# Filler matmuls on a cleared tile, from TensorE's first moment to the first keys, in a windowed-attention and squared-ReLU kernel

## The chip, the cores and the metric

The kernel runs on one core of a Trainium2 chip. The metric is the device time in microseconds (us); lower is better. Four runs of the kernel before gave 293.84, 294.88, 294.56 and 294.54 us, so the median is 294.55 us.

## What is computed

Causal attention with a window of 64 keys over 8 batches, 8 heads, 576 positions and 64 values a head, and then a feed-forward layer with a squared ReLU on its 4608 tokens:

```python
scores = scale * np.matmul(q, k.transpose(0, 1, 3, 2))
rel = pos[:, None] - pos[None, :]
mask = (rel >= 0) & (rel < window)            # window = 64
scores = np.where(mask, scores, -1000000000.0)
attn = softmax of scores
x = (attn @ v), heads side by side             # 4608 x 512
h = np.maximum(x @ w_in, 0.0)                  # w_in 512 x 2048
return (h * h @ w_out)                         # w_out 2048 x 512
```

(The softmax line and the line for x are shortened here.) All inputs and the output are float32; the kernel multiplies in float16.

## The kernel before, in words

**Tiling.** The 4608 tokens are 36 tiles of 128. Two tiles make a pair, four make a group of 512 tokens. A pair's q and k come by one DMA each (`fetch_pair`, L124), v by one DMA a tile (`fetch_v`, L149), all in float32. Each tile is cast to float16 (`cast_k`, `cast_q`, `cast_v`, L269 and L267), q and k are transposed on TensorE through the identity (`T`, L363) and copied out of PSUM (`copy_kT`, `copy_qT`). `S_` (L413) multiplies keys and queries. For the first four tiles it starts from a bias that holds the mask: two matmuls of the identity with `minus` (L417). `expo` (L430) takes the exponential on ScalarE, `V` (L441) multiplies with the values, `norm` (L452: `rden`, `x_sb`) divides by the row sum on VectorE, `X` (L464) transposes the result and `copy_xT` puts it in place as `xT`. `shift_v` makes the copy of v that is shifted by 64 rows (`v_od`). `U` (L492) is the first feed-forward product of a pair, `relu` and `square` follow, and `O` and `out_seven` make the second product.

**Order.** Nothing is scheduled by a planner in the stretch that matters here. The string `FIRST` (L17) lists the opening work by hand, from left to right: `fv3` is the fetch of v of tile 3, `kc1/D` the cast of k of tile 1 on VectorE (`/D`; `/A` is ScalarE, nothing is GpSimd), `Tk0` the transposes of k of pair 0, `ck0` their copy, `S0` the scores of tile 0, `ea0` and `eb0` its two halves of the exponential, `V0`, `n0`, `X0`, `x0` the later steps of tile 0, `w3.0` the scaling of one piece of w_in. Each engine takes its own instructions strictly in this order. All DMAs are issued on SP's queue, in this order too.

**Fillers.** `W` followed by a number calls `warm` (L541). It takes the next PSUM buffer of two pools in turn and issues that many matmuls into it whose results nobody reads. Each multiplies the identity with the first 256 columns of `mask_first`:

```python
for _ in range(n):
    nc.tensor.matmul(ps[:, 0:256], ident[:],
                     mask_first[:].rearrange("p a r -> p (a r)")[:, 0:256],
                     start=True, stop=True)
```

The list holds `W10` ahead of the first keys, `W1` between the first transposes of k and q, `W6` ahead of `S0`, `W2` after `S1`, `W5` between `V0` and `V1`, `W7` after `Tq1` and `W8` after `X0`: 39 filler matmuls. The identity comes from GpSimd (L223). `mask_first` comes from GpSimd's `base` (L224 to L233), a copy and a clearing on VectorE (L245, L249). Ahead of those, VectorE runs 19 small memsets (L192, L238 to L241).

Of the kernel before, what the change touches and what calls it, by code (L numbers as in the profile page):

```python
# [10 lines left out]
FP16 = mybir.dt.float16  # L11
# [3 lines left out]

SQ_ACT = (0, 1, 4, 6, 8, 10, 12, 14)
FIRST = '''  # L17
fv3 fk0 fq0 W10 fv0 kc1/D kc0 fq1 Tk0 W1 fv1 qc1/A qc0 vc3/A Tq0 W6 vc0/D h0 vd0 cq0 fv2 ck0 fk1
qc2/A S0 S1 W2 vc1 ea0 fw3 vd3 fw2 eb0 vd1/D ea1 fw1 V0 W5 qc3/D eb1 vc2 fw0 h2 n0 vd2 V1 Tq1 W7
n1 kc2/A kc3 cq1 Tk1 X0 W8 ck1 x0 X1 S2 x1/A fv4 w3.0 w3.3/A S3 w3.1 ea2 w3.2 eb2 U0.7 ea3 V2 eb3  # L20
w2.2 U0.6 w2.3/A n2 w2.0/A V3 w2.1 r0.7 X2 n3 U0.5 r0.6 s0.7/A x2 X3 h4 U0.4 r0.5 x3 fk2 w1.0
s0.6/A U1.7 w1.1 w1.3/A s0.5 U1.5 r0.4 r1.7/D s0.4/A fq2 U1.6 w1.2 r1.5 s1.7 w0.0/A U0.2 w0.2 vc4
# [18 lines left out]
def kernel(  # L41
# [9 lines left out]
    nc = tc.nc  # L51
    B, H, S, D = q.shape
    NT, DM = out.shape
    DFF = moe_w_in.shape[1]
    P = 128
# [13 lines left out]
    const = ctx.enter_context(tc.tile_pool(name="const", bufs=1))  # L69
# [116 lines left out]

    def as_stage(ap, c=4):
        return ap.bitcast(FP32).rearrange("p (c n) -> p c n", c=c)


    tick_of = smallp.tile([P, 16], FP32, name="tick", tag="tick", bufs=1)
    nc.vector.memset(tick_of[:, 0:1], 0.0)  # L192
    nc.scalar.activation(out=tick_of[:, 1:2], in_=tick_of[:, 0:1], func=AF.Exp)

    wb_stage = as_stage(wb_all[:, 0:2].rearrange("p i k n -> p (i k n)"))
    hs_stage = as_stage(hs_all[:].rearrange("p i k n -> p (i k n)"))
    w_in_stage = [as_stage(early[:, 0:8].rearrange("p f t -> p (f t)")),
                  as_stage(early[:, 8:16].rearrange("p f t -> p (f t)")),
                  wb_stage, hs_stage]
# [22 lines left out]
    ident = const.tile([P, P], FP16, name="ident")  # L222
# [20 lines left out]
    def make_mask(name, first=None):  # L243
        m = const.tile([P, HP * 2, 64], FP16, name=name)
        nc.vector.tensor_copy(out=m[:], in_=base[:].rearrange("p (o r) -> p o r", o=1)  # L245
                              .to_broadcast([P, HP * 2, 64]))
        if first is not None:
            mm = m[:].rearrange("p (a b) r -> p a b r", b=2)
            nc.vector.memset(mm[0:64, :, first, :], 0.0)  # L249
        return m  # L250

    mask_first = make_mask("mask_first", 0)
# [104 lines left out]
    def either_pool():  # L357
        turns.append(len(turns) % 2)
        return ((ps_up, "ps_u"), (ps_out, "ps_o"))[turns[-1]]
# [181 lines left out]
    def warm(n):  # L541
        pool, tag = either_pool()
        ps = pool.tile([P, 512], FP32, name="warm", tag=tag)
        for _ in range(n):
            nc.tensor.matmul(ps[:, 0:256], ident[:],
                             mask_first[:].rearrange("p a r -> p (a r)")[:, 0:256],
                             start=True, stop=True)

    def w_out_sum(k0, kind):
        ks, kl = slice(k0, k0 + 2), slice(KH + k0, KH + k0 + 2)  # L550
# [34 lines left out]
    def out_seven(g):  # L585
# [118 lines left out]
        "V": V, "n": norm, "X": X, "x": copy_xT,   # L704
        "U": U, "r": relu, "s": square, "O": O, "oe": out_copy, "st": out_store,
        "ws": lambda kind, k0: w_out_sum(2 * k0, kind), "W": warm,
    }
    engines = {"A": nc.scalar, "D": nc.vector, "P": nc.gpsimd}
# [129 lines left out]
```

## Time and profile before

| what | us |
|---|---|
| median of four runs | 294.55 |
| lowest and highest run | 293.84, 294.88 |
| the profiled execution, its own time | 293.84 |
| its span, first to last instruction | 292.1 |
| outside the span | 1.7 |

| engine | busy us | share of the span |
|---|---|---|
| TensorE (PE), matmuls | 283.4 | 97% |
| TensorE, weight loads (PEld) | 195.6 | 67% |
| VectorE (DVE) | 213.4 | 73% |
| ScalarE (ACT) | 192.1 | 66% |
| GpSimd (POOL) | 112.2 | 38% |

The profiled execution is the fastest of the four runs. All times inside the profile count from its first instruction. A row of the timeline gives the start, the length from the first start to the last end, the engine, the line, the operation, the tiles (written <- read), the shape and the number of instructions that were merged. A bracket at its end gives the time that the engine sat idle before it and what ended that. Matmuls overlap in the records: each one's length includes its way through the array, so the distance from one start to the next is what a matmul costs in a stream. The lines that carry the argument are shown in the prediction.

### The profile page before, as it was taken

How to read it: one execution, taken by the hardware profiler on the slowest of the kernel's cores; microseconds unless marked ns; L12 is line 12 of the kernel's file. 1: busy time of each engine (PE TensorE's matmuls, PEld its weight loads, DVE VectorE, ACT ScalarE, POOL GpSimd, SP SyncE). 2: the span in 40 equal slices, each digit the busy share in tenths (PEclk: the TensorE clock that was granted, in tenths of full speed). 3: DMA queues.
4: the chain of work that ended last, by engine and by line, in shares of the span. 5: the costliest groups of instructions: out<-in, count | busy, mean ns of one | idle time of the engine just before them, and what ended most of it. 6: DMA issues, size and time to landing. Idle time of an engine off the chain costs nothing.

```text
span 292.1 us, 7468 instructions
## 1 busy us (share of the span) xinstructions
PE 283.4 (97%) x3039; PEld 195.6 (67%) x3039; DVE 213.4 (73%) x392; ACT 192.1 (66%) x304; POOL 112.2 (38%) x171
## 2 busy tenths in 40 slices
PE   3999999999999999999999999999999999999995
PEld 2678888755666666666666666666666666666684
DVE  3679999869968677766777687768876876555393
ACT  2779898968676666756675767575758575666500
POOL 2602877667338603324655726251356300000000
PEclk9999999999999999999999999999999999999999
DMA  7999999999799378899999999799979901300133
GB/s 211 291 394 319 271 250 280 375 259 244 214 224 213 70 214 186 187 188 260 238 244 192 228 225 181 176 237 213 227 159 267 180 2 49 133 0 2 72 108 110
DMA packets 151842, 57.64 MB, mean 197 GB/s; under 512 B 128256, under 2 KB 143616, under 8 KB 151808
## 3 DMA queue, kind: packets, MB, share of 16 engines
q1 hardware_dynamic: 151808, 57.16, 80.6%
q8 instruction: 24, 0.39, 0.5%
q14 instruction: 10, 0.08, 0.1%
HBM read 38.80 MB, written 9.44 MB: 165 GB/s over the span
## 4 chain that ended last, share of the span: by engine, by line
PE 80%; DVE 10%; DMA 3%; ACT 3%; SPq 2%; issue 1%; POOL 0%; POOLq 0%
PE hps L526 30%; PE opsC L614 10%; PE opsD L614 8%; PE hps L498 7%; PE opsA L614 6%; PE ops L574 5%; PE opsB L614 4%; PE av L448 3%; DVE hs_all L602 3%; PE sc L425 2%; DVE pm L436 2%; DMA v_st<-in_v_dram 2%; DVE x_sb L457 1%; DMA xT<-x_sb 1%; PE xt_ps L468 1%; SPq L130 1%
## 5 line engine op out<-in xcount | busy, mean ns | idle before, releaser
L526 PE MATMUL hps<-xT,w_in_sb 128*128 128x512 f16 x448 | 112.9, 379 | 0.4 <-DVE h L536 0.2
L530 ACT ACTIVATE hrelu<-hps 128x512 f32<-128x512 f32 x112 | 66.7, 597 | 63.7 <-PE hps L526 63.1
L614 PEld LDWEIGHTS <-h 128*128 128x128 f16 x624 | 60.4, 98 | 20.8 <-issue 0.2
L526 PEld LDWEIGHTS <-w_in_sb 128*128 128x128 f16 x448 | 42.2, 98 | 33.6 <-issue 0.6
L536 DVE SCALAR_TENSOR_TENSOR h<-hps,hrelu 128x512 f16<-128x512 f32 x54 | 37.2, 689 | 32.6 <-ACT hrelu L530 32.4
L269 POOL COPY v_od<-v_ev 64x512 f16<-64x512 f16 x54 | 38.8, 718 | 5.3 <-ACT v_ev L267 1.4
L431 ACT ACTIVATE pm<-sc 128x1024 f16<-128x1024 f32 (+1 forms) x40 | 35.4, 941 | 3.7 <-PE sc L425 3.7
L533 ACT ACTIVATE h<-hrelu 128x512 f16<-128x512 f32 x58 | 36.5, 629 | 1.6
L614 PE MATMUL opsA<-w_out_sb,h 128*128 128x256 f16 x240 | 31.0, 273 | 0.0
L614 PE MATMUL opsD<-wb_all,h 128*128 128x256 f16 x240 | 30.9, 273 | 0.0
L614 PEld LDWEIGHTS <-hs_all 128*128 128x128 f16 x256 | 25.0, 98 | 8.6
L498 PE MATMUL hps<-xT,w_in_sb 128*128 128x256 f16 x256 | 30.1, 273 | 0.0
L498 PEld LDWEIGHTS <-w_in_sb 128*128 128x128 f16 x256 | 24.2, 98 | 2.9
L457 DVE TENSOR_TENSOR x_sb<-av,rden 128x512 f16<-128x512 f32 x36 | 24.9, 692 | 1.2
L436 DVE TENSOR_TENSOR pm<-pm,mask_inner 128x1024 f16<-128x1024 f16 x25 | 20.5, 824 | 5.6 <-ACT pm L431 5.6
L269 POOL CAST k<-kq_st 128x512 f16<-128x512 f32 x17 | 10.4, 614 | 33.1 <-DMA kq_st<-in_k_dram 32.8
L269 POOL CAST q<-kq_st 128x512 f16<-128x512 f32 x22 | 14.5, 658 | 18.8 <-DMA kq_st<-in_q_dram 18.7
L636 DVE SCALAR_TENSOR_TENSOR osb_all<-opsD,u 128x512 f32<-128x512 f32 x14 | 9.7, 692 | 11.2 <-PE opsD L614 11.1
L614 PE MATMUL opsC<-w_out_sb,h 128*128 128x256 f16 x128 | 16.4, 273 | 0.0
L614 PE MATMUL opsB<-wb_all,hs_all 128*128 128x256 f16 x128 | 16.4, 273 | 0.0
L614 PE MATMUL opsC<-w_out_sb,hs_all 128*128 128x256 f16 x128 | 16.4, 273 | 0.0
L269 POOL CAST v_ev<-kq_st 128x512 f16<-128x512 f32 x16 | 11.2, 698 | 11.4 <-DMA kq_st<-in_v_dram 10.9
(103 smaller groups left out, 371.2 us busy)
## 6 DMA issues: line engine op xcount, KB each, us to landing
kq_st<-in_k_dram SPq DMA_DIRECT2D x26, 256.0 KB, 3.9
kq_st<-in_v_dram SPq DMA_DIRECT2D x24, 256.0 KB, 4.1
out_dram<-osb_all SPq DMA_DIRECT2D x12, 512.0 KB, 4.3
kq_st<-in_q_dram SPq DMA_DIRECT2D x18, 256.0 KB, 4.3
v_st<-in_v_dram SPq DMA_DIRECT2D x16, 256.0 KB, 5.6
k_st<-in_k_dram SPq DMA_DIRECT2D x7, 512.0 KB, 6.0
q_st<-in_q_dram SPq DMA_DIRECT2D x7, 512.0 KB, 5.9
out_dram<-osb_all SPq DMA_DIRECT2D x11, 256.0 KB, 2.8
```

Of the source, the lines that this page charges most:

```text
L269: eng.tensor_copy(out=out, in_=in_)
L431: nc.scalar.activation(out=pms[i][:, part], in_=scs[i][:, part], func=AF.Exp, scale=1.0 / float(D) ** 0.5)
L436: nc.vector.tensor_tensor(out=pms[i][:, part], in0=pms[i][:, part], in1=mask[:].rearrange("p (o a) r -> p o (a r)", o=1) .to_broadcast([P, ...
L457: nc.vector.tensor_tensor(out=xs[i // 2][:, i % 2], in0=avs[i][:, :, :, 0:D], in1=rden[:].to_broadcast([P, 2, 4, D]), op=ALU.mult)
L498: nc.tensor.matmul(hps[:, f, :], w_in_sb[:, c, (2 * j + f) * P:(2 * j + f + 1) * P], xT_of(p // 2)[:, n0:n0 + 2, c, :], start=(c == 0), st ...
L526: nc.tensor.matmul(hps[:], w_in_sb[:, c, f * P:(f + 1) * P], xT_of(g)[:, :, c, :], start=(c == 0), stop=(c == DMC - 1))
L530: nc.scalar.activation(out=hrelu[:], in_=hps[:], func=AF.Relu)
L533: later(2 if f == 0 else 0, lambda: nc.scalar.activation(out=h2_of(g)[:, f, :], in_=hrelu[:], func=AF.Square))
L536: nc.vector.scalar_tensor_tensor(out=h2_of(g)[:, f, :], in0=hps[:], scalar=0.0, in1=hrelu[:], op0=ALU.max, op1=ALU.mult)
L574: nc.tensor.matmul(ops_of[ts][:], h2s[0][:, f, ts * P:(ts + 1) * P], w_out_sb[:, f, :], start=(f == 0), stop=(f == FFC - 1))
L614: nc.tensor.matmul(rows_of(bank, m), a[:, kk, m * P:(m + 1) * P], w[:, kk], start=(first and kk == 0 and (m == 0 or bank in apart)), stop= ...
L636: nc.vector.scalar_tensor_tensor(out=dst, in0=banks[bank][:, ms], scalar=OUT_SCALE, in1=sums[add][:, ms], op0=ALU.mult, op1=ALU.add)
```

## The change

The tile `idle` (128 x 256, float16) is new. VectorE clears it ahead of its other work. Every filler multiplies this tile by its own first 128 columns; it no longer reads the identity or `mask_first`. Three counts in the list change: `W10` becomes `W25`, `W6` becomes `W12` and `W2` becomes `W4`, so there are 62 fillers instead of 39.

```diff
-fv3 fk0 fq0 W10 fv0 kc1/D kc0 fq1 Tk0 W1 fv1 qc1/A qc0 vc3/A Tq0 W6 vc0/D h0 vd0 cq0 fv2 ck0 fk1
-qc2/A S0 S1 W2 vc1 ea0 fw3 vd3 fw2 eb0 vd1/D ea1 fw1 V0 W5 qc3/D eb1 vc2 fw0 h2 n0 vd2 V1 Tq1 W7
+fv3 fk0 fq0 W25 fv0 kc1/D kc0 fq1 Tk0 W1 fv1 qc1/A qc0 vc3/A Tq0 W12 vc0/D h0 vd0 cq0 fv2 ck0 fk1
+qc2/A S0 S1 W4 vc1 ea0 fw3 vd3 fw2 eb0 vd1/D ea1 fw1 V0 W5 qc3/D eb1 vc2 fw0 h2 n0 vd2 V1 Tq1 W7
...
+    idle = const.tile([P, 256], FP16, name="idle")
+    nc.vector.memset(idle[:], 0.0)
+
+
     tick_of = smallp.tile([P, 16], FP32, name="tick", tag="tick", bufs=1)
     nc.vector.memset(tick_of[:, 0:1], 0.0)
...
-            nc.tensor.matmul(ps[:, 0:256], ident[:],
-                             mask_first[:].rearrange("p a r -> p (a r)")[:, 0:256],
-                             start=True, stop=True)
+            nc.tensor.matmul(ps[:, 0:256], idle[:, 0:P], idle[:], start=True, stop=True)
```

In the built program the order of all other instructions stays as it was on every engine. From the first `out_seven` on, the sums `p1` and `u` take other ones of the five slots that they share with the v tiles.

## The prediction

> **What bounds the kernel now.** I read the page first: busy time and slices.
>
> ```profile
> PE 283.4 (97%) x3039; PEld 195.6 (67%) x3039; DVE 213.4 (73%) x392; ACT 192.1 (66%) x304; POOL 112.2 (38%) x171
> ...
> PE   3999999999999999999999999999999999999995
> ...
> PEclk9999999999999999999999999999999999999999
> ```
>
> TensorE is busy from the second slice to the end, so the time is its stream plus its start. The change touches only the start. PEclk says full clock throughout, yet the timeline of the first 18 us shows that TensorE is not at full speed there:
>
> ```profile
> 2.72 2.29 PE L545 MATMUL warm<-mask_first,ident 128*128 128x256 f16 x10 [2.72 <-DVE mask_first L249]
> ...
> 6.97 1.03 PE L373 MATMUL kT_ps<-ident,k 128*128 128x128 f16 x8 [1.96 <-POOL k L269]
> ...
> 8.23 1.03 PE L373 MATMUL qT_ps<-ident,q 128*128 128x128 f16 x8
> ...
> 9.05 1.49 PE L545 MATMUL warm<-mask_first,ident 128*128 128x256 f16 x6
> ...
> 10.33 0.75 PE L417 MATMUL sc<-osb_all,ident 128*128 128x512 f16 x2
> ...
> 11.36 0.61 PE L417 MATMUL sc<-osb_all,ident 128*128 128x512 f16 x2
> ...
> 14.01 0.62 PE L373 MATMUL qT_ps<-ident,q 128*128 128x128 f16 x8
> ...
> 17.19 0.38 PE L468 MATMUL xt_ps<-ident,x_sb 128*128 128x128 f16 x4 [0.23 <-DVE xT L269]
> ```
>
> Eight transposes take 1.03 us at 6.97 and 8.23 but 0.62 at 14.01: from start to start 0.107 us against 0.056. A 256-column filler costs 0.213 us up to 10.33 and 0.109 from 12.24 on. So TensorE runs at half speed until about 10.65 (inside the pair of 10.33, whose first matmul takes 0.374 instead of 0.216), some 3.7 us after the transposes began. The burst of 2.72 to 4.80 was too short to end the half speed.
>
> Then I read who waits. The waits of TensorE in the first 60 us are three, two of them before any useful work:
>
> ```profile
> PE warm L545 <- DVE mask_first L249: 2.7, 1, 2.7
> PE kT_ps L373 <- POOL k L269: 2.0, 1, 2.0
> PE xt_ps L468 <- DVE xT L269: 0.2, 1, 0.2
> ```
>
> The third, at 17.19, is the last time that TensorE waits before its dense stream. The chain leads there, and not through the slow matmuls:
>
> ```profile
> 6.07 4.85 DMA v_st<-in_v_dram
> ...
> 11.04 0.62 POOL v_ev L269
> ...
> 11.68 0.28 DVE v_od L269
> ...
> 15.63 1.21 DVE qT L269
> 16.84 0.31 DVE xT L269
> ...
> 17.19 0.38 PE xt_ps L468 x4
> ```
>
> The v of tile 1 lands at 10.92. GpSimd casts it, and VectorE works ten instructions in a row without idling, 11.68 to 17.14, the last being `x0`. X1 starts 0.05 later. From 17.19 to 35 us the stream has no other gap but about 0.095 us where matmuls of another shape begin.
>
> **The change part by part.**
>
> *Clearing.* 128x256 float16 has the size of the kT memset at 8.87 (128x128 words, 0.17 us). It runs at 0.88, where VectorE's first memset stood, so the first filler starts at 0.88 + 0.17 + 0.05 = 1.10 instead of 2.72. Every early VectorE instruction moves by at most 0.17; the last ends near 3.4 instead of 3.21, and the next waits for a DMA until 6.02. Nothing of this is paid. If that cover were gone, it would cost 0.17. No DMA, no GpSimd and no SP instruction is moved.
>
> *W25.* At half speed 25 x 0.213 = 5.33 us, ending at 6.43. The keys are cast at 6.91, so this fits with 0.5 us to spare. If the clock rises 3.4 to 3.7 us after 1.10, as it did after 6.97, that is at 4.5 to 4.8: 16 or 17 fillers at 0.213, eight or nine at 0.109, ending near 5.6.
>
> *What rises.* [...] By the row alone (3.7 us after a start) TensorE is fast from 4.8. [...]
>
> *What is fast then.* The transposes of q still wait for GpSimd's cast until 8.23. They end 8 x (0.107 - 0.056) = 0.41 sooner, and VectorE's `cq0` starts at 9.04 instead of 9.30 (behind its memset). W12 costs 12 x 0.109 = 1.31, from 8.67 to 9.98, where W6 cost 1.28 and ended at 10.33. The bias pair costs 0.43 instead of 0.59. S0 starts near 10.51 instead of 11.02, the exponentials 0.5 sooner, W4 adds 2 x 0.109 = 0.22 while V0 waits for them, and V0 and V1 come about 0.5 sooner. Then it ends: k of tile 2 is cast at 14.15 when its DMA lands and k of tile 3 by 15.19 on GpSimd, so Tk1 gains 0.17 at most; X1 waits for `x0` at 17.14 as before. The wait at X1 grows from 0.40 to about 0.5. S2 follows X1. So against the profiled execution, 293.84, the sum is zero.
>
> *Where a gain remains.* The profiled execution is the fastest of four; the median is 0.71 above. [...] Slow work after 10.65 costs about half its length. [...] I take this for the main cause of the spread; this one trace cannot show it. With TensorE fast before 8 us in every run, the loss is gone: near 293.84, plus 0.15 for what else varies. Forecast 294.0. The bounds of this term are 0 (the spread has other causes) and -1.0 (the slowest run's whole excess).
>
> *Later slots.* The sums take other slots from 78 us on; the last v tile is read by 69.9, so no wait comes from it: zero.
>
> **The rivals.**
>
> *No change, 294.55.* The loss is hidden anyway: by the chain view VectorE and the v transfer set 17.19, and the spread comes from DMAs. For it: the chain as shown. [...] Range 294.2 to 294.9.
>
> [...]
>
> [...]
>
> **How the numbers follow.** Cases: gone spread 0.60 (own range 293.5 to 294.4), no change 0.25, window in the pause 0.09, zeros 0.06. About 0.3% (0.88 us) is what a measurement of this kernel can tell from no change, so faster means below 293.67 and slower above 295.43. Faster: a third of the first case, 0.20. Slower: the zeros and a remainder, 0.08. The range 293.4 to 294.9 takes in the first three and leaves out the last.
>
> **What would show it.** In the profile after: the first filler at 1.10 and W25 over before 6.5; transposes at 6.97 within about 0.62 us; S0 near 10.5; X1 still waiting for VectorE's `xT` near 17.2, with a longer wait; everything later as before; and runs that lie closer together. I am wrong if X1 comes clearly sooner, if the transposes at 6.97 take 1.03, or if the runs spread as before.

## The result, and the profile after

The changed kernel takes 294.0 us (median of 35 runs, 292.65 to 296.5), the kernel before 294.8 us in the same comparison (56 runs, 293.33 to 296.45). The ratio is 0.9982, 95% interval [0.9968, 0.9997]. That is a small gain, within the 0.3% that the prediction called no change; 294.0 was forecast. A second comparison (experiment 8) gave 0.9988 and does not rule out no change at all. The profiled execution took 293.67 us, its span is 291.8 us.

The timeline of the changed kernel over its first 20 us, its TensorE rows, beside those of before:

```profile
1.13 5.37 PE L549 MATMUL warm<-idle 128*128 128x256 f16 x25 [1.13 <-DVE tick L196]
...
6.59 0.62 PE L377 MATMUL kT_ps<-ident,k 128*128 128x128 f16 x8
...
7.89 0.62 PE L377 MATMUL qT_ps<-ident,q 128*128 128x128 f16 x8 [0.58 <-POOL q L273]
...
8.35 1.47 PE L549 MATMUL warm<-idle 128*128 128x256 f16 x12
...
10.19 0.41 PE L429 MATMUL sc<-qT,kT 64*128 64x64 f16 x16
...
16.74 0.38 PE L472 MATMUL xt_ps<-ident,x_sb 128*128 128x128 f16 x4 [0.24 <-DVE xT L273]
```

The fillers begin at 1.13 instead of 2.72. Eight transposes take 0.62 us at once, where they took 1.03: the clock rose at 6.22, just before the last of the 25 fillers, and was up for the keys. (The trace keeps a record of the clock's changes, which begins at the first rise; the times of rises and falls below are from it. The kernel before has its rise at 10.64.) S0 starts at 10.19 instead of 11.02. X1, the row at the bottom, still waits for VectorE's `xT`. The waits of TensorE up to 60 us:

```profile
PE warm L549 <- DVE tick L196: 1.1, 1, 1.1
PE qT_ps L377 <- POOL q L273: 0.6, 1, 0.6
PE xt_ps L472 <- DVE xT L273: 0.2, 1, 0.2
```

The last one, at X1, is as long as before. (The first is put down to `tick`; the fillers wait for the memset just before it.) The chain of waits up to 17 us shows what decides X1:

```profile
3.99 1.66 SPq L130
...
5.70 4.76 DMA v_st<-in_v_dram
...
10.58 0.62 POOL v_ev L273
...
11.23 0.29 DVE v_od L273
...
15.17 1.22 DVE qT L273
16.38 0.31 DVE xT L273
...
16.74 0.38 PE xt_ps L472 x4
```

It is the chain of before, link by link, and it starts earlier: SP was busy 1.66 us with the fetch of q of pair 1 instead of 2.09, so the v of tile 1 was issued at 5.70 instead of 6.07, and GpSimd began its cast at 10.58 instead of 11.04. From that cast to X1 it is 6.15 us before and 6.16 after. So the 0.45 us by which X1 comes sooner in this pair of profiles is the transfer's, not TensorE's; S2 follows 0.22 us behind X1 in both. The two profiles alone would have misled: the clock changed as planned, and the change of X1 that stands beside it has another cause.

### The profile page after: what moved, and what is told of

Read it like the earlier page. It is cut to its first block, busy times and chain, and to the rows that moved or that the text cites. A ratio compares the mean times of both kernels' runs of the same rounds, so it can differ in the third digit from the quotient of the medians.

```text
span 291.8 us, 7514 instructions
## 1 busy us (share of the span) xinstructions
PE 285.8 (98%) x3062; PEld 197.4 (68%) x3062; DVE 214.4 (73%) x393; ACT 192.2 (66%) x304; POOL 111.7 (38%) x171
## 4 chain that ended last, share of the span: by engine, by line
PE 82%; DVE 8%; SPq 3%; DMA 3%; issue 1%; ACT 1%; POOL 0%; POOLq 0%
PE hps L530 31%; PE hps L502 9%; PE opsC L616 9%; PE opsD L616 8%; PE opsA L616 7%; PE opsB L616 4%; PE av L452 3%; PE sc L429 3%; PE ops L576 3%; SPq L121 2%; DVE x_sb L461 2%; DMA v_st<-in_v_dram 2%; DVE hs_all L604 1%; DMA xT<-x_sb 1%; DVE pm L440 1%; PE xt_ps L472 1%
## 5 line engine op out<-in xcount | busy, mean ns | idle before, releaser
L273 POOL COPY v_od<-v_ev 64x512 f16<-64x512 f16 x54 | 37.7, 698 | 6.6 <-ACT v_ev L271 2.7
L502 PE MATMUL hps<-xT,w_in_sb 128*128 128x256 f16 x256 | 30.1, 273 | 0.0
```

What stands on the lines that cost most here:

```text
L273: eng.tensor_copy(out=out, in_=in_)
L502: nc.tensor.matmul(hps[:, f, :], w_in_sb[:, c, (2 * j + f) * P:(2 * j + f + 1) * P], xT_of(p // 2)[:, n0:n0 + 2, c, :], start=(c == 0), st ...
```

## The experiments

The theory: the gain is a full clock by the first keys, which spares those executions in which the clock rises late. Against it: the early start or the cleared tile is worth something in itself, or DMAs make all the differences. What the theory says of S2 can be read in a profile as the time from GpSimd's cast of v of tile 1 to S2, which leaves out how late that v landed. The first four kernels ran on one chip (before there: 294.44, 67 runs), the next four on one chip too (before: 294.27, 75 runs).

**1. The cleared tile alone, counts of before.**

```diff
-fv3 fk0 fq0 W25 ... Tq0 W12 ... S1 W4
+fv3 fk0 fq0 W10 ... Tq0 W6 ... S1 W2
```

> The cleared tile alone, with the counts of before (10, 6, 2). Clock theory (the gain is a full TensorE clock when the first keys come): ten fillers end near 3.3 us, too short for the clock to rise, the transposes of k at about 6.9 still take 1.03 us, the rise comes near 10.4 to 13.8, and the time is that of before, ratio 1.000 +- 0.001. Rival (an early start of TensorE is worth something in itself, or fillers no longer wait for the mask): ratio 0.998, as the whole change.

294.45 us, ratio 1.0002 [0.9982, 1.0022]: no gain. Its timeline:

```profile
1.14 2.31 PE L549 MATMUL warm<-idle 128*128 128x256 f16 x10 [1.14 <-DVE tick L196]
...
6.52 1.03 PE L377 MATMUL kT_ps<-ident,k 128*128 128x128 f16 x8 [3.07 <-POOL k L273]
...
7.76 1.04 PE L377 MATMUL qT_ps<-ident,q 128*128 128x128 f16 x8
...
15.56 0.61 PE L377 MATMUL kT_ps<-ident,k 128*128 128x128 f16 x8
...
16.21 1.32 ACT L271 ACTIVATE kT<-kT_ps 128x1024 f16<-128x1024 f16 x1 [1.89 <-PE kT_ps L377]
...
17.10 0.39 PE L472 MATMUL xt_ps<-ident,x_sb 128*128 128x128 f16 x4
...
17.58 0.59 PE L421 MATMUL sc<-osb_all,ident 128*128 128x512 f16 x2
```

The ten fillers are over 3 us before the keys; both sets of transposes run at half speed, and the clock rises at 12.10 (inside the second bias pair, whose matmuls start at 11.41 and 11.81). The same steps in the profile before, with the rise at 10.64:

```profile
15.23 0.61 PE L373 MATMUL kT_ps<-ident,k 128*128 128x128 f16 x8
...
15.88 1.31 ACT L267 ACTIVATE kT<-kT_ps 128x1024 f16<-128x1024 f16 x1 [1.10 <-PE kT_ps L373]
...
17.41 0.59 PE L417 MATMUL sc<-osb_all,ident 128*128 128x512 f16 x2
```

Counted from the cast of v of tile 1 (10.66 here, 11.04 before), Tk1 comes at 4.90 instead of 4.19, its copy `ck1` on ScalarE moves with it, and S2, the bottom row, starts at 6.92 instead of 6.37, right behind `ck1`, which ends at 17.53. In the changed kernel S2 is at 6.38 (16.96 less 10.58). A late clock costs 0.55 us here, and starting early is worth nothing by itself.

**2. 32 opening fillers.**

```diff
-fv3 fk0 fq0 W25 fv0
+fv3 fk0 fq0 W32 fv0
```

> [...] The changed kernel's 35 runs lie in two groups, 23 from 292.65 to 294.5 and 12 from 294.8 to 296.5. [...] Rival (the spread comes from the DMAs, such as the landing of the v of tile 1): the spread stays, median 294.0, a third of the runs above 294.7.

293.0 us (22 runs, 292.62 to 294.55), ratio 0.9969 [0.9951, 0.9987]. No run lies above 294.7, where the rival had a third of them, and the median is 1.0 below the 294.0 that it gave. (The expectation counts 12 runs in the upper group; there are 13.) The clock rose at 5.82. Standard deviation of the runs: 0.66 us, against 0.91 of before beside it. The interval overlaps with that of 25 fillers, so that 32 are better than 25 is likely and not shown.

**3. The new counts with the old operands.**

```diff
-fv3 fk0 fq0 W10 ... Tq0 W6 ... S1 W2
+fv3 fk0 fq0 W25 ... Tq0 W12 ... S1 W4
```

> The new counts (25, 12, 4) with the old operands, so that the fillers begin at 2.72 us. Clock theory: 25 fillers run up to the first keys and hold TensorE until 7.6 to 8.0, which costs nothing since the copies of kT and qT wait for ScalarE and VectorE until 8.58 and 9.04; the clock rises at 6.1 to 9.6, and the time is that of the changed kernel or lower, 293.4 to 294.0, with no upper group. Rival (the early start matters, not the length of the burst): no better than before, 294.8; or above it by up to 0.5 since the first transposes come late.

293.54 us (22 runs, 292.48 to 294.96), ratio 0.9968 [0.9952, 0.9984]: the gain is all there without the cleared tile and the early start. Its fillers begin at 2.72 and end into the keys:

```profile
2.72 5.49 PE L545 MATMUL warm<-mask_first,ident 128*128 128x256 f16 x25 [2.72 <-DVE mask_first L249]
...
8.01 0.93 PE L373 MATMUL kT_ps<-ident,k 128*128 128x128 f16 x8
...
8.88 0.61 PE L373 MATMUL qT_ps<-ident,q 128*128 128x128 f16 x8
...
17.31 0.38 PE L468 MATMUL xt_ps<-ident,x_sb 128*128 128x128 f16 x4
```

The clock rose at 8.66. The first transposes come over a microsecond late and mostly at half speed, and nobody minds: X1 is 6.15 after the cast at 11.16, as with a full clock before the keys.

**4. No fillers.** All seven `W` words are taken out of the changed kernel's list.

> No fillers at all: what the clock is worth. Clock theory: TensorE stays at half speed until its dense stream has run for 3.4 us or more, to about 21 to 24 us; X1 still starts near 17.2 since VectorE and the v transfer set it, and about half of 4 to 7 us is lost after it: 296.5 to 298. Rival (the clock in the opening does not matter): 294 to 295.

296.69 us (22 runs, 293.87 to 299.64), ratio 1.0068 [1.0044, 1.0091]. Without any filler the kernel takes some 2.2 us more than with the 39 of before. The profiled execution is the shortest of the 22; the clock rose at 15.99 in it, not at 21 to 24 as expected, and X1 is 6.83 and S2 7.05 after the cast (10.38). That the slower executions had a still later rise fits the theory, but no trace shows it.

**5. 16 opening fillers.**

```diff
-fv3 fk0 fq0 W25 fv0
+fv3 fk0 fq0 W16 fv0
```

> [...] Clock theory: the transposes at 6.6 to 7.0 take 1.03 us, the twelve fillers ahead of S0 run at half speed for most of their length, S0 comes near 11 to 12, X1 late, and nearly all runs look like the upper third of the changed kernel's: median 295.3, ratio 1.003 to before. Rival (only the total number of fillers or the cleared tile counts): 294.0.

294.56 us (22 runs), ratio 1.0009 [0.9991, 1.0026]: the gain is gone, though not turned into the loss of 0.3% that I expected, and the runs spread from 293.24 to 296.57. The expectation was also wrong on the first transposes. Timeline:

```profile
1.13 3.60 PE L549 MATMUL warm<-idle 128*128 128x256 f16 x16 [1.13 <-DVE tick L196]
...
6.75 0.62 PE L377 MATMUL kT_ps<-ident,k 128*128 128x128 f16 x8 [2.02 <-POOL k L273]
...
8.46 1.03 PE L377 MATMUL qT_ps<-ident,q 128*128 128x128 f16 x8 [0.98 <-POOL q L273]
...
9.29 2.68 PE L549 MATMUL warm<-idle 128*128 128x256 f16 x12
```

The transposes of k at 6.75 are at full speed, those of q at 8.46 at half: the clock rose at 4.92, at the start of the pause, and fell again at 8.33. Three stretches that end at the changes of the clock (columns: stretch, sum, busy time of TensorE with its instructions, of its weight loads and of the other engines, the granted clock, the DMA share and rate):

```profile
1.50:4.92 3.42, 3.23 (x16) 1.98 (x13) 1.62 (x12) 0.80 (x2) 0.48 (x2) 1.00 0.89 233
4.92:8.33 3.41, 0.73 (x9) 0.51 (x9) 0.43 (x1) 0.56 (x2) 1.40 (x2) 1.00 1.08 292
8.33:11.74 3.41, 3.28 (x20) 2.60 (x21) 1.87 (x3) 2.41 (x4) 1.41 (x4) 0.50 1.01 254
```

The changes lie 3.41 us apart. In the first stretch TensorE was busy for 3.23 us, and the clock rose at its end. In the second it was busy for 0.73, and the clock fell. In the third it was busy for 3.28, and it rose again, at 11.74. The stretch ahead of the fall was not idle throughout. (The 1.00 of the first row means that no change was on record yet; the fillers there are 0.213 us apart, half speed.)

**6. 32 fillers, and v of tile 1 fetched ahead of q of pair 1.**

```diff
-fv3 fk0 fq0 W25 fv0 kc1/D kc0 fq1 Tk0 W1 fv1 qc1/A
+fv3 fk0 fq0 W32 fv0 kc1/D kc0 fv1 Tk0 W1 fq1 qc1/A
```

> 32 opening fillers, and the fetch of the v of tile 1 issued ahead of that of q of pair 1. In all profiles with a full clock so far X1 starts 6.15 us after GpSimd begins the cast of that v. Chain theory: the cast begins at about 10.3, as soon as GpSimd is done with v of tile 0, X1 comes near 16.4, and part of it is given back where w_in lands: 292.7, ratio 0.996 to before, 0.2 to 0.4 below the kernel with 32 fillers alone. Rival (q of pair 1, 0.7 us later, becomes the late one and holds S2): 293.0 or above.

The cast began at 9.94 and X1 came at 16.39, the earliest of all profiles: it does follow that transfer. But it is 6.45 behind the cast, no longer 6.15: it starts right behind the fillers W8, without a wait for VectorE. And S2 starts at 16.86, behind `ck1`, which ends at 16.80. Against experiment 2, X1 gained 0.39 us and S2 only 0.14. The time is 293.97 us (22 runs), ratio 0.9989 [0.9971, 1.0007], no better than with 32 fillers alone. The waits of its TensorE from 12 to 60 us show new ones:

```profile
PE qT_ps L377 <- ACT q L271: 0.3, 1, 0.3
PE kT_ps L377 <- POOL k L273: 0.3, 1, 0.3
```

They are at 31.1 and 30.1, at the transposes of pair 2: GpSimd cast its second k tile there at 29.43, after 28.63 in the profile of experiment 2. That is some 0.6 us lost, and not where I had placed it (where w_in lands: VectorE waited there for 0.87 us, TensorE did not). It need not come from the new order: in one execution of the changed kernel, with its fetches in the old order, that cast began at 29.63 and TensorE waited 0.2 us for q.

**7. 32 opening fillers, the others as before.**

```diff
-fv3 fk0 fq0 W25 ... Tq0 W12 ... S1 W4
+fv3 fk0 fq0 W32 ... Tq0 W6 ... S1 W2
```

> 32 opening fillers, the other counts as before (6 and 2). Clock theory: once the clock is up at the first keys, the longer fillers only fill waits, S0 comes near 9.7 by the wait for qT, X1 as before, 293.0, equal to the kernel with 32, 12 and 4. Rival (the longer fillers keep the clock up through the waits between 8 and 12): the clock falls again or rises late, 294 or more.

293.31 us (22 runs), ratio 0.9968 [0.9949, 0.9986]: the same as with 12 and 4. The longer later fillers are not what brings the gain. In its profiled execution a late cast of k of pair 1 held Tk1 (1.20 us of waiting, until 16.08), so its X1, 17.64, says nothing of the clock, which rose at 5.76.

**8. The changed kernel again.** Once beside experiments 5 to 7, and three single executions for their profiles.

> The changed kernel as it is, on the chip of the three others. Clock theory: two groups again, about a third of the runs above 294.7, median 293.7 to 294.0, between the kernel with 16 fillers and the one with 32. Rival (the two groups were an accident of the first chip): one group.

293.7 us (22 runs, 292.26 to 295.94), ratio 0.9988 [0.9970, 1.0006]: between 16 and 32 fillers, as said. Five of 22 runs lie above 294.7, not a third, and there are no two groups to be seen.

> The changed kernel again, one look for its profile. Both looks at it so far had the clock up before the keys (6.2 and 5.7 us). [...]

> As the look before it: about one in three with the clock late, X1 then more than 6.3 us after the cast of v of tile 1 begins, else 6.15.

> As the two looks before it: about one in three with the clock late, X1 then more than 6.3 us after the cast of v of tile 1 begins, else 6.15. If none of the three shows it, the share of such phases is smaller than the changed kernel's upper third of runs, and that third has another cause in part.

The three took 293.99, 294.05 and 293.44 us. With the two earlier profiles these are five of the changed kernel. The clock rose at 6.22, 5.66, 6.44, 5.06 and 4.21, always before the keys, and X1 came 6.15 or 6.16 us after the cast of v of tile 1 in each. None shows a late clock; how the opening goes with a rise later than 6.44, they do not show. The cast itself began at 10.58, 10.61, 11.32, 11.02 and 10.51.

## Why the prediction was right, and where not

**The number and its cause hold.** 294.0 was forecast and measured; so close a match is luck, with an interval of some 0.4 us to either side and 293.7 in the second comparison. That the clock is the cause is shown by the experiments and not by the pair of profiles: too short a burst gives nothing (1.0002, and 1.0009 with 16), a burst that lasts to the keys gives the gain, from zeros or not (0.9969, 0.9968, 0.9968; the changed kernel itself 0.9982 and 0.9988), and no burst costs 0.68%. The profiles agree: with fetches in the old order and no late k, S2 comes 6.37 to 6.41 us after the cast of v of tile 1 in all eight in which the clock was up by 10.64 and stayed up, and 6.92, 7.05 and 7.11 in the three in which it was not (experiments 1, 4 and 5).

**The steps inside the profile hold.** First filler 1.10 forecast, 1.13 measured; W25 over before 6.5 (the last one starts at 6.23 and its row ends at 6.50); transposes 0.62; S0 0.5 sooner at equal transfers (10.51 forecast, 10.19 measured with transfers 0.37 earlier); X1 bound by VectorE, 6.15 us behind the cast of v of tile 1. "Against the profiled execution the sum is zero" holds to 0.01 us on that distance. Only the wait at X1 did not grow: TensorE came to X0 sooner and waited there, for VectorE's `n1`, which writes the same tile `x_sb` and ended at 15.17, so that X0 (15.22), W8 and X1 kept their distance from it.

**The term that gave the gain is shown for one rise; how often it is paid is not.** The forecast takes away the 0.71 us between the lowest run and the median, as the price of a late clock, and adds 0.15; no run shows that a late clock costs the median run this much. What the runs show: in experiment 1, with the counts of before and a rise at 12.10, Tk1 is 0.71 late, about half of the 1.46 us between its rise and that at 10.64, and S2, behind `ck1`, is 0.55 late. In experiment 5 S2 is 0.74 late (18.73, cast at 11.62), in experiment 4, with the rise at 15.99, 0.68 (17.43, cast at 10.38). How often the kernel before sees which rise, no run shows. A gain of 0.31% is 0.9 us, more than any of these three delays, and no trace shows where the rest comes from.

**Two of my signs of being wrong came.** X1 came clearly sooner, by 0.45 us; the fixed distance to the cast shows that the transfer did that. And the runs do not lie closer together: the changed kernel's have a standard deviation of 1.12 us against 0.74 of before in the first comparison, 0.92 against 0.86 in the second. I had read the 0.71 us between the lowest run and the median as the clock's and called it the main cause of the spread. The runs speak against that: the least spread of all, 0.54 us (14 runs), is that of experiment 1, where ten fillers leave the clock late; experiments 2, 3 and 7 have 0.66, 0.63 and 0.67. One other part is the transfers': the cast of v of tile 1 began anywhere from 10.38 to 11.62 in the profiles with an unchanged list of fetches, and X1 follows it. Another lies behind the opening: in the five profiles of the changed kernel S2 starts between 16.89 and 17.70, but from there to the end it takes from 273.3 to 274.8 us, a wider range. What makes that second part vary is open.

**Half wrong: the pause.** That the pause ahead of the keys does not bring the half speed back was my estimate. It held in five executions of five, but in experiment 5, with pauses of 2.02 and 0.98 us and only the transposes of k and one filler between them, the clock fell at 8.33. That 13 of the first 35 runs of the changed kernel lay above 294.7 looked like this case. The five profiles do not show it, and in the second comparison these runs were five of 22. What held those 13 runs up stays open.

**Zeros, the case with 0.06, did not come.** The clock rose at 5.82 behind fillers of zeros (experiment 2) and at 8.66 behind fillers of an identity and a mask (experiment 3), 4.68 and 5.94 us after the first filler.

## What to carry to other kernels

A filler burst ahead of the first data pays here if it lasts until the data come; its length in microseconds and the pause behind it count, not its early start nor its data. Ten or sixteen fillers that stopped 2 to 3 us before the keys brought nothing, and 25 to 32 that ran up to them brought 0.1 to 0.3%. Before crediting such a change with a difference between two profiles, measure the distance from the transfer that bounds the opening to the first wait of the dense stream: here it was 6.15 us with and without the change, while its start moved by a microsecond from run to run. And take several profiles of each kernel: what the change removes, a rise later than 10.64, the one profile of the kernel before did not show.

## What the hardware showed that I had not expected

The granted clock reads 1.00 in the profile's rows before the first recorded change, even where matmuls of 256 columns are 0.213 us apart, and 0.50 only where a fall was recorded (experiment 5). The distances of starts, or the time of the first entry in the trace's record of the clock, are the surer sign at the head of a kernel.

From its rise on, the clock stayed up for 283.31 us in the kernel before and for 286.72 us in the changed one, by the trace's record: until 293.95 and 292.94, after the last matmul, which ends at 288.89 and 288.60. The two lengths differ by 3.41 us, as far as the changes of experiment 5 lie apart.

How much work lies ahead of a change, the traces show for these cases. TensorE was busy in the 3.41 us ahead of a rise for 3.40 us in the kernel before (1.4 of transposes, 1.8 of fillers and the bias, counted by their starts), for 3.41 in the changed one, and for 3.23 and 3.28 in experiment 5. In experiment 3 fillers alone ran for 2.53 us, from 2.72 to 5.25, and the clock rose only 3.41 us later. Once up, it stayed up in the changed kernel over 2.75 us of busy time in the 3.41 us behind the rise at 6.22, and over 1.96 behind that at 5.06 (experiment 8); in experiment 5 it fell at the end of 3.41 us with 0.73. How much it takes, no run shows. The pauses: 0.58 us ahead of the transposes of q (the profile after) and 0.40 and 0.52 ahead of those of k and of q (experiment 8) did no harm, the 2.02 and 0.98 us of experiment 5 did.
